# Decode attention with a gated feed-forward: TensorE's loop body as half a set used twice, with one value slot

## The chip, the cores and the metric

The kernel runs on one core of a Trainium2 chip. The metric is device time in microseconds of one execution; the median of three runs before the change is 195.83 us (195.80 to 195.85). One more execution was taken with the hardware profiler, and its page and trace are what the text quotes. Engines are named as on that page: PE (TensorE matmuls), PEld (its weight loads), DVE (VectorE), ACT (ScalarE), POOL (GpSimd), SP (SyncE, which only issues transfers here).

## The reference

Four batch rows, one token each. The output is a gate between sliding-window attention over a cache and a gated feed-forward:

```python
g = sigmoid((x * gate_w).sum(-1, keepdims=True))
# attention: 32 query heads, 8 key/value heads, the last W = 4096 of 16384 positions, Dh = 128
q = (x @ wq)                                  # per head
p = softmax(q @ k.T * Dh ** -0.5)             # over W positions
a = (p @ v) @ wo
# feed-forward, F = 1792
gate = x @ W_gate; up = x @ W_up
b = (gate * (gate > 0) * up) @ W_down
return g * a + (1 - g) * b
```

All inputs are bf16. The keys and values that are read are 4 batches x 8 heads x 4096 positions x 128 each, 32 MiB of keys and 32 MiB of values; with the weights the core reads 81 MB.

## The kernel before, in words

The work is cut into eight sets. A set is one batch and four key/value heads: its keys are one 4 MiB load, its values another. Loads go to `slots`, four buffers of 128 x 16384 bf16. `_dma_order` lists the loads as SP issues them, on one queue: wq, x, gate_w, k0, k1, v0, then k(s) and v(s-1) in turn, then the two feed-forward weights wg and wu (which share a slot), v7, wd, and wo in five pieces. `_slots` hands out the four buffers in rotation and notes what a load waits for: the last reader of what lay there before. A key slot is free when DVE has evicted score block 2 of its set (by then all four transposes have read it), a value slot after the value products `PV`. SP issues in order, so a load that waits holds up all loads behind it.

A set's work, with the names that the code uses:

- `KT(s, f)`, f = 0 to 3 (L555): DVE transposes a quarter of the keys from the slot into `kt`, which has four buffers of 128 x 4096, one for each f.
- `SC(s, f)`: TensorE makes a block of scores, 8 matmuls of 512 columns, into one of four PSUM banks (`SCB`), then DVE evicts the block with a running maximum (`ESC`, L591).
- after block 3: `MAX` and `SW` (a 32-column matmul) with `ESW` on DVE (L601) give the negated maximum; `EXP` on ACT (L694) makes the exponentials into `pe` with their sums.
- `PT(s)` (`EPT`, L606): DVE transposes them into `pT`, which has two buffers, used in turn.
- `PV(s)`: 32 matmuls of `pT` with the values, into one of two PSUM banks (`OB`), copied out by ACT (`NORM`, L679).

After the loop TensorE does the row sums (`RS`), the feed-forward's first products (`GU`), the last `PV`, then `FFN`, the mix of the heads (`OQ`) and the output projection `WO`, piece by piece as wo lands. All matmuls are recorded under one helper line, L306.

`_order` fixes one sequence of these steps, from which DVE's and ACT's programs are made. TensorE's program is written apart, as blocks with branches: a block `set` (score blocks 0 to 2 of a set), then `even` or `odd` (the value products of the set before, one copy for each value semaphore and `pT` buffer), then `rest` (score block 3 and `SW`); `setup` and `gates` are run once, `mix` and `tail` end it. TensorE waits for semaphores that DVE raises (`kt`, `mx`, `pt`), that ACT raises (`nm`) and that the value loads raise (`d_v0`, `d_v1`). In this order the value products of set s-1 stand between score blocks 2 and 3 of set s, and DVE does the first transpose of set s before it evicts block 3 of set s-1:

```python
for s in range(1, NSET):
    o += [("KT", s, 0), ("SC", s - 1, 3), ("SW", s - 1)]
    o += [("KT", s, 1), ("PT", s - 1), ("SC", s, 0), ("KT", s, 2), ("SC", s, 1), ("KT", s, 3)]
    o += [("SC", s, 2), ("PV", s - 1)]
```

Of the kernel before, what the change touches and what calls it, by code (L numbers as in the profile page):

```python
# [104 lines left out]
def _alloc(nc, ctx):  # L105
# [42 lines left out]
def _order():  # L148
    o = [("CONST", k) for k in ("mask", "grp", "rfold")] + [("XT",), ("Z",), ("Q",), ("QT",), ("KT", 0, 0), ("KT", 0, 1), ("SC", 0, 0)]
    o += [("KT", 0, 2), ("SC", 0, 1), ("KT", 0, 3), ("SC", 0, 2)]  # L150
    for s in range(1, NSET):
        o += [("KT", s, 0), ("SC", s - 1, 3), ("SW", s - 1)]
        o += [("KT", s, 1), ("PT", s - 1), ("SC", s, 0), ("KT", s, 2), ("SC", s, 1), ("KT", s, 3)]
        o += [("SC", s, 2), ("PV", s - 1)]
    s = NSET - 1
    o += [("SC", s, 3), ("SW", s), ("PT", s), ("RS", 0), ("RS", 1), ("GU",), ("PV", s), ("FFN",), ("OQ",)]
    return o + [("WO", p) for p in range(len(WO_PIECES))]
# [9 lines left out]
def _slots():  # L167

    frees = [[] for _ in range(NSLOT)]
    at, wait = {}, {}  # L170
    turn = 0
    for it in _dma_order():
        k = it[0]
        if k in ("x", "gw") or (k == "wo" and it[1] > 0):
            continue
        if k == "wu":
            at[it] = at[("wg",)]
            wait[it] = wait[("wg",)]
            continue
        n = turn % NSLOT  # L180
        turn += 1
        at[it] = n
        wait[it] = list(frees[n])
        frees[n] = {"k": [("E", "SC", it[-1], 2)], "v": [("PV", it[-1])], "wq": [("Q", 1)], "wg": [("GU", 1)], "wd": [], "wo": []}[k]
    return at, wait


def _program(nc, plan, R, aps):
    (A_x, A_k_cache, A_v_cache, A_wq, A_wo, B_W_gate, B_W_up, B_W_down, gate_w, out) = aps
    banks = [R["psum"][:, i, :] for i in range(8)]  # L190
# [29 lines left out]
    free = {("RS", 0): [("E", "SW", NSET - 1)], ("RS", 1): [("E", "SC", NSET - 1, 0)], ("GU", 0): [("E", "SC", NSET - 1, 1)],  # L220
            ("GU", 1): [("E", "SC", NSET - 1, 2)], ("OQ",): [("E", "SC", NSET - 1, 3)], ("Q", 0): [("INIT",)], ("Q", 1): [("INIT",)]}
    for i, key in enumerate(turns):
# [12 lines left out]

    def ob(s):
        return banks[OB[s % 2]]

    def sync(e):
# [5 lines left out]
        for it in _dma_order():  # L245
# [19 lines left out]
            else:  # L265
                b, qq = set_of(it[1])
                src = (A_k_cache if k == "k" else A_v_cache)[b, 4 * qq:4 * qq + 4, SK - WIN:SK, :]
                load((k.upper(), it[1]), f"d_{k}{it[1] % (3 if k == 'k' else 2)}", slot(*it), src.rearrange("h (r c) d -> r h (c d)", r=32),
                     waits=w)
# [32 lines left out]
    def tensor(t):  # L302
# [46 lines left out]
        def SC(s, f, s_at=0):  # L349
            key = ("SC", s, f)  # L350
            bk = banks[scb(key)]
            kv = kt[:, f, :].rearrange("p (t c h k e) -> p t c h k e", t=2, c=16, h=2, k=32)
            if plan.emit:
                E.take("kt", f + 1, 4 if f == 3 else 0)
            for t in range(2):
# [17 lines left out]
        def PV(s):  # L373
            vv = slot("v", s).rearrange("p (f t c d) -> p f t c d", f=4, t=2, c=16)
            if plan.emit:
                E.take("nm", 1, 1)
                E.take("pt", 1, 1)
                E.take(f"d_v{s % 2}", 16, 16)
            for f in range(4):
                for c in range(0, 16, 2):  # L380
                    x = 512 * f + 32 * c
                    r = 64 * (c // 2 % 2)
                    mm(ob(s)[r:r + 64, :], pT[:, s % 2, x:x + 64], vv[:, f, :, c:c + 2, :], (f, c) in ((0, 0), (0, 2)),
                       (f, c) in ((3, 12), (3, 14)), ev=("PV", s) if (f, c) == (3, 14) else None, pos=(0, r))

        def OQ():
            key = ("OQ",)
            if plan.emit:
                E.take("nm", 2)
            for t in range(2):  # L390
# [45 lines left out]
        if not plan.emit:  # L436
            setup()
            for s in range(NSET):
                for f in range(3):
                    SC(s, f)  # L440
                if s:
                    PV(s - 1)
                SC(s, 3)
                SW(s)
# [9 lines left out]

        at, odd = t.alloc_register("at"), t.alloc_register("odd")
        t.reg_mov(at, 0)
        t.reg_mov(odd, 1)
        t.sem_inc(plan.sems["nm"], 2)
        here = t.mark_branch_hint_location()
        t.br("pe_setup")  # L460
        with block("set"):
            sv = t.snap(at, min_val=0, max_val=NSET - 1)
            for f in range(3):
                SC(0, f, sv)
            t.br_eq(at, 0, on_true="pe_rest", on_false="pe_turn")
        with block("turn"):
            t.br_eq(odd, 0, on_true="pe_even", on_false="pe_odd")
        with block("even"):
            PV(0)
            t.br("pe_rest")  # L470
        with block("odd"):
            PV(1)
            t.br_eq(at, NSET, on_true="pe_mix", on_false="pe_rest")
        with block("rest"):
            SC(0, 3, t.snap(at, min_val=0, max_val=NSET - 1))
            SW(0)
            t.reg_add(at, at, 1)
            t.reg_alu(odd, odd, 1, op=ALU.bitwise_xor)
            t.br_lt(at, NSET, on_true="pe_set", on_false="pe_leave")
        with block("leave"):  # L480
            t.br("pe_gates")
        E.seen = {}
        with block("gates"):
            run("RS", "GU")
            t.br("pe_odd")
        E.seen = {}
        with block("setup"):
            setup()
            t.br("pe_set")
        E.seen = {}  # L490
# [55 lines left out]
    def vector(v):  # L546
        E = _Eng(plan, v, "dve")

        def INIT():
            E.op(lambda: v.memset(qblk[:, :, :, :, :].rearrange("p s h c e -> p (s h c e)"), 0.0), ev=("QZ",))  # L550
            E.op(lambda: v.memset(R["psum"][:, SCB[1]:ACC + 1, :].rearrange("p k c -> p (k c)"), 0.0), ev=("INIT",))

        def EKT(s, f):
            w = [("K", s)] + ([("SC", s - 1, f)] if s else [])
            E.op(lambda: v.transpose(kt[:, f, :].bitcast(FP32), slot("k", s)[:, 4096 * f:4096 * f + 4096].bitcast(FP32)),  # L555
                 ev=("E", "KT", s, f), waits=w, ctr="kt")
# [48 lines left out]
        def EPT(s):  # L605
            E.op(lambda: v.transpose(pT[:, s % 2, :], pe[:, :]), ev=("E", "PT", s), ctr="pt",  # L606
                 waits=[("EXP", s)] + ([("PV", s - 2)] if s >= 2 else [("XT",)]))

# [51 lines left out]
    def scalar(a):  # L660
# [17 lines left out]
        def NORM(s):  # L678
            E.op(lambda: a.activation(osb[:, s, :], ob(s), ACTF.Copy), ev=("NORM", s), ctr="nm",  # L679
                 waits=[("PV", s)])  # L680
# [53 lines left out]
```

## Time and profile before

| what | us |
|---|---|
| median of three runs | 195.83 |
| the profiled execution, its own time | 195.97 |
| its span, first to last instruction | 194.7 |
| DVE busy | 124.4 |
| PE busy | 124.0 |
| 32 key transposes on DVE | 73.7 |
| 256 score matmuls on PE | 72.0 |
| 256 value matmuls on PE | 32.3 |

The page gives busy time, then the span in 40 slices (busy tenths of each engine, the granted TensorE clock in tenths, the DMA engines' share, GB/s), the DMA queues, and the costliest groups. The timeline lists instructions in order of time: start, length, engine, line, operation, output and input, count, and in brackets the idle time ahead of it with what ended that. The windows give a row for each stretch: its bounds and length, then busy time and count for PE, PEld, DVE, ACT and POOL, then the granted clock, the DMA share and GB/s.

### The profile page before, as it was taken

The page shows a single profiled execution, that of the slowest core. Times are in us where ns is not written, and L with a number is a line of the kernel's source. Part 1 is how long each engine was busy: PE and PEld are TensorE (multiplying, and loading weights), DVE is VectorE, ACT ScalarE, POOL GpSimd, SP SyncE. Part 2 cuts the span into 40 slices and gives each one's busy share as a digit, 9 for nine tenths or more (in the row PEclk, how much of TensorE's full clock was granted, in tenths as well). Part 3 has the DMA queues.
Part 4 walks back from the last instruction along what each step waited for, and adds up shares of the span by engine and source line. Part 5 has one row for each costly group of instructions (what it writes and reads, how often), then busy time and mean ns, then how long its engine had stood idle before and what let it go on. Part 6 is the DMA issues. An engine that isn't in the chain of part 4 may idle for free. (4 is left out here: it accounts for less than half of the span.)

```text
span 194.7 us, 1963 instructions
## 1 busy us (share of the span) xinstructions
PE 124.0 (64%) x723; PEld 53.0 (27%) x723; DVE 124.4 (64%) x153; ACT 27.5 (14%) x34; POOL 9.6 (5%) x25
## 2 busy tenths in 40 slices
PE   0209257573966696579358627863886398764975
PEld 0004222131422242124113212321232133232563
DVE  6103688999489829991998099809980998253010
ACT  2213100040022004101310131013101300150100
POOL 7830000000000000000000000000000000000000
PEclk9999859998899579969999988995799669978699
DMA  6999999999999999999999999999999999998991
GB/s 222 427 439 438 431 431 431 451 438 438 431 431 431 431 431 438 431 438 431 431 438 431 438 431 431 431 431 438 431 431 431 431 385 424 477 438 380 432 396 58
DMA packets 3619, 81.03 MB, mean 416 GB/s; under 512 B 409, under 2 KB 674, under 8 KB 802
## 3 DMA queue, kind: packets, MB, share of 16 engines
q1 hardware_dynamic: 3618, 81.01, 97.2%
q8 instruction: 1, 0.02, 0.0%
HBM read 81.01 MB, written 0.00 MB: 416 GB/s over the span
## 5 line engine op out<-in xcount | busy, mean ns | idle before, releaser
L555 DVE STREAM_TRANSPOSE kt<-slots 128x2048 f32<-128x2048 f32 x32 | 73.7, 2305 | 25.1 <-DMA slots<-in_A_k_cache_dram 25.1
L306 PE MATMUL bank<-kt,qblk 128*128 128x512 bf16 x256 | 72.0, 432 | 27.6 <-DVE kt L555 22.5
L306 PEld LDWEIGHTS bank<-kt,qblk 128*128 x256 | 25.8, 107 | 69.4 <-issue 27.3
L306 PE MATMUL bank<-slots,pT 128*64 128x512 bf16 x256 | 32.3, 410 | 2.8 <-PEq L82 2.8
L591 DVE CUSTOM_DVE_ANT_0 sc<-bank,maskf 128x512 bf16<-128x512 f32 x32 | 21.1, 660 | 7.8 <-PE bank L306 7.8
L694 ACT ACTIVATE pe<-sc,negmax 128x2048 bf16<-128x2048 bf16 x8 | 16.0, 2002 | 50.4 <-DVE negmax L601 50.4
L306 PEld LDWEIGHTS bank<-slots,pT 128*64 128x64 bf16 x256 | 15.4, 118 | 20.5 <-issue 10.7
L606 DVE STREAM_TRANSPOSE pT<-pe 128x2048 bf16<-128x2048 bf16 x8 | 18.5, 2312 | 2.2 <-ACT pe L694 2.2
L679 ACT ACTIVATE osb<-bank 128x512 bf16<-128x512 f32 x8 | 4.8, 597 | 90.1 <-PE bank L306 90.1
L306 PE MATMUL bank<-rd,grpb 128*128 128x32 bf16 x8 | 1.4, 179 | 20.6 <-PEq L82 20.6
L306 PEld LDWEIGHTS bank<-rd,grpb 128*128 128x128 bf16 x8 | 0.8, 98 | 24.3 <-issue 24.3
L619 DVE TENSOR_TENSOR oq<-bank,recip 64x128 bf16<-64x128 f32 x2 | 0.9, 434 | 9.7 <-PE bank L306 9.7
L306 PE MATMUL bank<-slots,xT 128*4 128x512 bf16 (+1 forms) x64 | 6.5, 583 | 0.0
L559 DVE COPY xT<-bank 128x20 bf16<-128x20 bf16 x1 | 0.2, 170 | 7.7 <-PE bank L310 7.7
L306 PE MATMUL bank<-slots,oq 128*4 128x256 bf16 x64 | 4.3, 272 | 1.3 <-DVE oq L619 1.1
L581 DVE TENSOR_SCALAR qblk<-bank 32x64 uint32<-32x64 uint32 x16 | 2.9, 215 | 3.0 <-PE bank L310 2.9
L306 PE MATMUL bank<-maskr,maskl 128*128 128x512 bf16 x1 | 0.6, 606 | 5.9 <-POOL maskr L282 5.9
L310 PE MATMUL bank<-identb,xsb 5*128 5x5 bf16 x4 | 0.3, 167 | 5.6 <-DMA xsb<-in_A_x_dram 5.6
L306 PEld LDWEIGHTS bank<-slots,oq 128*4 128x4 bf16 x64 | 2.7, 84 | 2.9 <-DMA slots<-in_A_wo_dram 2.4
L282 POOL TENSOR_SCALAR_AFFINE_SELECT fold<-fold 128x256 bf16<-128x256 bf16 x8 | 3.4, 419 | 1.1
L641 DVE CAST xsb<-bank 4x256 bf16<-4x256 f32 x1 | 0.4, 419 | 4.7 <-PE bank L306 4.7
L601 DVE TENSOR_REDUCE negmax<-bank 128x1 f32<-128x32 f32 x8 | 1.5, 191 | 2.9 <-PE bank L306 2.9
(59 smaller groups left out, 42.3 us busy)
## 6 DMA issues: line engine op xcount, KB each, us to landing
slots<-in_A_k_cache_dram SPq DMA_DIRECT2D x8, 4096.0 KB, 24.1
slots<-in_A_v_cache_dram SPq DMA_DIRECT2D x8, 4096.0 KB, 30.6
slots<-in_A_wq_dram SPq DMA_DIRECT2D x1, 4096.0 KB, 13.6
slots<-in_A_wo_dram SPq DMA_DIRECT2D x1, 2240.0 KB, 21.1
slots<-in_B_W_gate_dram SPq DMA_DIRECT2D x1, 1792.0 KB, 19.0
slots<-in_B_W_up_dram SPq DMA_DIRECT2D x1, 1792.0 KB, 22.9
slots<-in_B_W_down_dram SPq DMA_DIRECT2D x1, 1792.0 KB, 17.9
slots<-in_A_wo_dram SPq DMA_DIRECT2D x1, 1088.0 KB, 23.4
```

The lines of the kernel that those rows point to most:

```text
L282: op(lambda: e.affine_select(dst, src, pattern, cmp, fill, base=base, channel_multiplier=mult), ev)
L306: E.op(lambda: t.matmul(out_, lhsT, rhs, start=start, stop=stop, tile_position=pos, skip_group_check=True), ev=ev, waits=waits)
L310: E.op(lambda: t.transpose(out_, in_, idn), ev=ev, waits=waits)
L555: E.op(lambda: v.transpose(kt[:, f, :].bitcast(FP32), slot("k", s)[:, 4096 * f:4096 * f + 4096].bitcast(FP32)), ev=("E", "KT", s, f), wait ...
L581: E.op(lambda dst=dst, r=r, g=g: v.tensor_scalar(dst, src[r, g, 0:B, :, :], 0, None, op0=ALU.bitwise_or), ev=("E",) + keys[1] if (q, g) == ...
L591: E.op(lambda: v.tensor_tensor_reduce(sc[:, 512 * f:512 * f + 512], banks[scb(key)], R["maskf"][:, :], 1.0, -3.0e38, ALU.add, ALU.max, mx4 ...
L601: E.op(lambda: v.tensor_reduce(negmax[:, s % 2:s % 2 + 1], banks[tr(key)][:, 0:32], AXIS.X, ALU.min), ev=("E",) + key, waits=[key])
L606: E.op(lambda: v.transpose(pT[:, s % 2, :], pe[:, :]), ev=("E", "PT", s), ctr="pt", waits=[("EXP", s)] + ([("PV", s - 2)] if s >= 2 else [ ...
L619: E.op(lambda g=g, r=r: v.tensor_tensor(oq[r, :, :].rearrange("p i b -> p b i"), banks[tr(key)][0:64, 128 * g:128 * g + 128].rearrange("p ...
L641: E.op(lambda: v.tensor_copy(osum[:, OW:2 * OW], banks[ACC][OR:OR + 4, 0:OW]), ev=("OSUM", 1), waits=[("WOP", len(WO_PIECES) - 1)])
L679: E.op(lambda: a.activation(osb[:, s, :], ob(s), ACTF.Copy), ev=("NORM", s), ctr="nm", waits=[("PV", s)])
L694: E.op(lambda: a.activation(pe[:, :], sc[:, :], ACTF.Exp, bias=negmax[:, s % 2:s % 2 + 1], scale=SCALE, accum_out=rowsum[:, s:s + 1]), ev= ...
```

## The change

TensorE's loop body becomes half a set: one block `half` with two score blocks, used twice for each set, with `value` (the value products) between the two halves. So `kt` has two buffers in place of four, the scores use two PSUM banks in place of four, `pT` has one buffer and the value products one accumulator bank. The value products of set s-1 stand ahead of score block 2 of set s, and DVE does the first transpose of set s after `SW` of set s-1. The fourth slot is for values alone and the other three go round among all other loads, so value load s waits for `PV(s-1)`; one semaphore `d_v` counts all value loads.

```diff
-    sb("kt", [128, 4, 4096], BF16)
+    sb("kt", [128, 2, 4096], BF16)
-    sb("pT", [128, 2, 2048], BF16)
+    sb("pT", [128, 2048], BF16)
...
-    o += [("KT", 0, 2), ("SC", 0, 1), ("KT", 0, 3), ("SC", 0, 2)]
+    o += [("KT", 0, 2), ("SC", 0, 1), ("KT", 0, 3), ("SC", 0, 2), ("SC", 0, 3), ("SW", 0)]
     for s in range(1, NSET):
-        o += [("KT", s, 0), ("SC", s - 1, 3), ("SW", s - 1)]
-        o += [("KT", s, 1), ("PT", s - 1), ("SC", s, 0), ("KT", s, 2), ("SC", s, 1), ("KT", s, 3)]
-        o += [("SC", s, 2), ("PV", s - 1)]
+        o += [("KT", s, 0), ("KT", s, 1), ("PT", s - 1), ("SC", s, 0), ("KT", s, 2), ("SC", s, 1), ("KT", s, 3), ("PV", s - 1)]
+        o += [("SC", s, 2), ("SC", s, 3), ("SW", s)]
...
-        n = turn % NSLOT
-        turn += 1
+        if k == "v":
+            n = NSLOT - 1
+        else:
+            n = turn % (NSLOT - 1)
+            turn += 1
...
-    TR, SCB, ACC, OB = (0, 1), (1, 2, 3, 4), 5, (6, 7)
+    TR, SCB, ACC, OB = (0, 1), (2, 3), 5, 6
...
-            bank_of[("SC", s, f)] = SCB[f]
+            bank_of[("SC", s, f)] = SCB[f % 2]
...
             if plan.emit:
-                E.take("kt", f + 1, 4 if f == 3 else 0)
+                E.take("kt", 1, 1)
...
-                E.take(f"d_v{s % 2}", 16, 16)
+                E.take("d_v", 16, 16)
...
+        with block("setup"):
+            setup()
+            t.br("pe_half")
         with block("turn"):
             SW(0)
             t.reg_add(at, at, 1)
+            t.br_lt(at, NSET, on_true="pe_half", on_false="pe_gates")
         with block("gates"):
             run("RS", "GU")
+            t.br("pe_value")
+        with block("half"):
+            sv = t.snap(at, min_val=0, max_val=NSET - 1)
+            for f in range(2):
+                SC(0, f, sv)
+            t.reg_alu(half, half, 1, op=ALU.bitwise_xor)
+            t.br_eq(half, 0, on_true="pe_turn", on_false="pe_first")
+        with block("first"):
+            t.br_eq(at, 0, on_true="pe_half", on_false="pe_value")
+        with block("value"):
+            PV(0)
+            t.br_lt(at, NSET, on_true="pe_half", on_false="pe_mix")
...
-            w = [("K", s)] + ([("SC", s - 1, f)] if s else [])
+            w = [("K", s)] + ([("SC", s, f - 2)] if f > 1 else [("SC", s - 1, f + 2)] if s else [])
...
-                 waits=[("EXP", s)] + ([("PV", s - 2)] if s >= 2 else [("XT",)]))
+                 waits=[("EXP", s)] + ([("PV", s - 1)] if s else []))
```

More of the change, by code (lines that the diff above doesn't have):

```diff
@@ L234, in set_of @@
         return s % 4, s // 4
-    def ob(s):
-        return banks[OB[s % 2]]
+    ob = banks[OB]
     def sync(e):
@@ L438, in tensor @@
             for s in range(NSET):
-                for f in range(3):
+                for f in range(4):
+                    if s and f == 2:
+                        PV(s - 1)
                     SC(s, f)
-                if s:
-                    PV(s - 1)
-                SC(s, 3)
                 SW(s)
@@ L453, in block @@
             return nc.body("pe_" + name, valid_engines=only)
-        at, odd = t.alloc_register("at"), t.alloc_register("odd")
+        at, half = t.alloc_register("at"), t.alloc_register("half")
         t.reg_mov(at, 0)
-        t.reg_mov(odd, 1)
-        t.sem_inc(plan.sems["nm"], 2)
+        t.reg_mov(half, 0)
+        t.sem_inc(plan.sems["nm"], 1)
         here = t.mark_branch_hint_location()
         t.br("pe_setup")
[L461 to L465, printed above, removed]
-        with block("turn"):
[L467 to L475, printed above, removed]
+        with block("setup"):
+            setup()
+            t.br("pe_half")
+        E.seen = {}
+        with block("turn"):
             SW(0)
             t.reg_add(at, at, 1)
[L478 to L481, printed above, removed]
+            t.br_lt(at, NSET, on_true="pe_half", on_false="pe_gates")
         E.seen = {}
```

29 lines of the change are left out of this document (12 added, 17 removed).

## The prediction

> **What bounds the kernel now.** I read the page's busy shares and slices first, then its DMA queues, then the windows, then the timeline around one set of the loop.
>
> ```profile
> span 194.7 us, 1963 instructions
> ...
> PE 124.0 (64%) x723; PEld 53.0 (27%) x723; DVE 124.4 (64%) x153; ACT 27.5 (14%) x34; POOL 9.6 (5%) x25
> ...
> PEclk9999859998899579969999988995799669978699
> DMA  6999999999999999999999999999999999998991
> ...
> q1 hardware_dynamic: 3618, 81.01, 97.2%
> q8 instruction: 1, 0.02, 0.0%
> ...
> slots<-in_A_k_cache_dram SPq DMA_DIRECT2D x8, 4096.0 KB, 24.1
> slots<-in_A_v_cache_dram SPq DMA_DIRECT2D x8, 4096.0 KB, 30.6
> ...
> slots<-in_B_W_gate_dram SPq DMA_DIRECT2D x1, 1792.0 KB, 19.0
> ```
>
> No engine is busy more than 64% of the span, while the 16 DMA engines are busy 97.2% of it, in every slice but the first and last few. The windows give the same by stage, and two short ones show the very end:
>
> ```profile
> 53.28:150.43 97.15, 66.72 (x343) 26.21 (x337) 70.32 (x76) 14.06 (x16) 0.00 (x0) 0.89 1.00 432
> 150.43:178.57 28.14, 17.40 (x102) 6.97 (x103) 19.67 (x27) 5.33 (x6) 0.00 (x0) 0.82 1.00 429
> ...
> 191.00:191.60 0.60, 0.60 (x16) 0.50 (x11) 0.00 (x0) 0.00 (x0) 0.00 (x0) 1.00 0.06 25
> 191.60:192.20 0.60, 0.60 (x12) 0.29 (x8) 0.00 (x0) 0.00 (x0) 0.00 (x0) 1.00 0.06 21
> ```
>
> The last two columns are DMA share and GB/s. Over five sets the share is 1.00 at 432 GB/s. In the last 1.2 us before 192.2 it is 0.06, one sixteenth: one DMA engine works alone, so every transfer lands when this late engine is done, and the other fifteen have over 1.2 us to spare. So the kernel's time is its bytes through the late engine, as long as the queue always holds the next transfer. A change in TensorE's order can cost something only where it lets that queue run dry. How far ahead the queue is filled is read from one set:
>
> ```profile
> 92.14 2.31 DVE L555 STREAM_TRANSPOSE kt<-slots 128x2048 f32<-128x2048 f32 x1 [4.37 <-DMA slots<-in_A_k_cache_dram]
> 94.37 0.65 DVE L591 CUSTOM_DVE_ANT_0 sc<-bank,maskf 128x512 bf16<-128x512 f32 x1
> ...
> 95.62 0.19 DVE L601 TENSOR_REDUCE negmax<-bank 128x1 f32<-128x32 f32 x1 [0.36 <-PE bank L306]
> 95.73 2.30 DVE L555 STREAM_TRANSPOSE kt<-slots 128x2048 f32<-128x2048 f32 x1
> ...
> 97.97 2.31 DVE L606 STREAM_TRANSPOSE pT<-pe 128x2048 bf16<-128x2048 bf16 x1
> ...
> 100.80 2.31 DVE L555 STREAM_TRANSPOSE kt<-slots 128x2048 f32<-128x2048 f32 x1
> 103.03 0.65 DVE L591 CUSTOM_DVE_ANT_0 sc<-bank,maskf 128x512 bf16<-128x512 f32 x1
> 103.16 1.91 PE L306 MATMUL bank<-kt,qblk 128*128 128x512 bf16 x8 [3.16 <-DVE kt L555]
> 103.61 2.31 DVE L555 STREAM_TRANSPOSE kt<-slots 128x2048 f32<-128x2048 f32 x1
> 105.00 3.64 PE L306 MATMUL bank<-slots,pT 128*64 128x512 bf16 x32
> ...
> 106.53 0.53 SPq L243 DMA_DIRECT2D slots<-in_A_k_cache_dram  x1
> 108.68 0.53 SPq L243 DMA_DIRECT2D slots<-in_A_v_cache_dram  x1
> 111.57 2.31 DVE L555 STREAM_TRANSPOSE kt<-slots 128x2048 f32<-128x2048 f32 x1 [5.07 <-DMA slots<-in_A_k_cache_dram]
> ```
>
> Keys land at about 92.14 and 111.57, 19.43 us apart, one key and one value load of equal size (4096 KB each by the issue rows), so a value load lands about 9.7 us behind its keys. At 106.53 and 108.68 the SP queue issues the loads that follow, while the key load landing at 111.57 and a value load landing about 121.3 are still under way: the queue is filled some 13 us ahead.
>
> **The change part by part.** Call T the landing of a set's keys.
>
> *One value slot.* Value load s now waits for the products of set s-1, and all loads behind it on SP's queue (the next keys, in the end wg, wu, wd, wo) wait with it. In the old order it waited for the products two sets back. The new key loads wait for a set three back and are never last. The step is nothing if the value products end early enough ahead of T+19.43, when the next keys are through. With the rows above, DVE does first and second transposes, pT, then eviction and transpose twice. A transpose is 2.23 from start to start (100.80 to 103.03), an eviction 0.58 (103.03 to 103.61): kt 0 and 1 until T+4.5, pT until T+6.7, kt 2 until T+9.5, kt 3 until T+12.3. TensorE does score blocks 0 and 1 by T+6.5 (1.91 each) and then waits for values: they land at T+9.7. Products 3.64: T+13.4. Score blocks 2 and 3 now stand behind them: T+17.2. From the last eviction to the end of negmax is 1.4 (94.37 to 95.73): T+18.6. That is 0.8 short of 19.43, so DVE is back in time for the next keys, with one accumulator bank (its copy runs while TensorE waits anyway) and one pT (needed again only at T+19.43+4.5).
>
> The next value load is issued at T+13.4, 6.0 us ahead of the end of the keys under way. How long a load needs to start isn't shown; the output's bounds it:
>
> ```profile
> 193.43 0.29 SPq L243 DMA_DIRECT2D out_dram<-xsb  x1
> ```
>
> From that issue to the end of the span are 1.3 us, landing included. So the lead falls from 13 to 4.7 us, but not to zero: 0 us lost per set.
>
> *Half clock.* A second cost could come from TensorE's clock, in tenths in the PEclk row. One block of scores and the products are seen slow as well:
>
> ```profile
> 47.32 3.29 PE L306 MATMUL bank<-kt,qblk 128*128 128x512 bf16 x8 [3.16 <-DVE kt L555]
> ...
> 178.57 5.33 PE L306 MATMUL bank<-slots,pT 128*64 128x512 bf16 x32 [2.82 <-PEq L82]
> ```
>
> A score block rises from 1.91 to 3.29, the products from 3.64 to 5.33, at worst twice 3.64 = 7.3. With 7.3 a value load is issued at T+17.0 and runs by T+18.3: still ahead of T+19.43. [...]
>
> *The first hand-over is the tight one.* Set 0 has no values to wait for, and DVE is behind the keys there:
>
> ```profile
> 33.49 2.31 DVE L555 STREAM_TRANSPOSE kt<-slots 128x2048 f32<-128x2048 f32 x1
> ...
> 36.10 1.91 PE L306 MATMUL bank<-kt,qblk 128*128 128x512 bf16 x8 [1.15 <-PEq L82]
> 36.30 2.31 DVE L555 STREAM_TRANSPOSE kt<-slots 128x2048 f32<-128x2048 f32 x1
> 36.41 0.54 SPq L243 DMA_DIRECT2D slots<-in_A_v_cache_dram  x1
> ...
> 51.38 0.53 SPq L243 DMA_DIRECT2D slots<-in_A_k_cache_dram  x1
> 53.28 2.31 DVE L555 STREAM_TRANSPOSE kt<-slots 128x2048 f32<-128x2048 f32 x1 [1.93 <-DMA slots<-in_A_k_cache_dram]
> ```
>
> Value load 1 went out at 36.41. Now: kt 3 of set 0 ends at 35.8, score block 3 at 37.9, negmax at 39.4. Only then come the transposes of set 1 (one of them ran at 36.30): until 43.9, pT until 46.2, products 46.3 to 49.9. Value load 1 goes out at 50.0 and runs by 51.3; the keys ahead of it (set 2) end at 53.28. That leaves 2.0 us: cost 0. If score blocks 0 and 1 of set 1 both run at 3.29 (41.7 to 48.3), the products end between 52.0 and 53.7, the load runs by 53.3 to 55.0, and 0 to 1.7 us are lost once. I take 0.1, nearer to the full clock, since TensorE worked at 36 and works from 41.7 on.
>
> *Fewer instructions, other jumps.* Counted in the code, with a weight load for each matmul, TensorE's program shrinks from 647 instructions to 538; a set takes five branches for four, and a score block takes its semaphore down by itself. A set's TensorE time has no share in the sum, so these cost 0; without that cover some 0.1 us a set.
>
> *The tail.* The last value load (behind wg and wu) is issued at 150.43+13.4 = 163.8; the queue holds v6, wg and wu until about 150.4+9.7+8.5 = 168.6 (wg and wu at 1792 of 4096 KB each take 4.25). wo moves to the slot of the last keys and waits for score block 2 (about 166) instead of the products:
>
> ```profile
> 164.84 0.33 SPq L243 DMA_DIRECT2D slots<-in_B_W_down_dram  x1
> ...
> 166.98 2.23 SPq L243 DMA_DIRECT2D slots<-in_A_wo_dram  x5
> ...
> 190.78 2.15 PE L306 MATMUL bank<-slots,oq 128*4 128x256 bf16 x29 [0.20 <-DMA slots<-in_A_wo_dram]
> ```
>
> Both were and are issued far ahead of the last value landing (178.5, where the products start at 178.57). The last matmuls still wait for the last piece of wo: 0.
>
> **Sum.** The profiled execution took 195.97 us (span 194.7 and 1.3 around it), 0.14 above the median of three. 195.97 + 0 + 0.1 = 196.07, against the median 195.83 + 0.1 = 195.9.
>
> **Rivals.**
> - B, the first hand-over runs dry (slower). TensorE's products of set 0 end after 52.0 because of the half clock, as worked out above; it decides from an issue of value load 1 later than 52.0. For it: the 3.29 of the old block at 47.32. Against: denser work there now. Price 0.4 to 1.7, so 196.2 to 197.5; 196.6 as the likeliest, since both blocks would have to be slow throughout for more.
> - C, the value slot binds in every set (slower). A set loses what its products end later than T+18.1 (19.43 less 1.3). It needs half clock through the products and both score blocks behind them: products until T+17.0, blocks until T+23.6, negmax T+25.0, 5.6 behind the next keys; pT is then ready 12.3 behind them, and products of 7.3 end at 19.6, 1.5 late. For it: the slow rows above. Against: the window 53.28:150.43 has a mean clock of 0.89 (third column from the end), so that half clock lasts a fifth of the time and not through. At 0.4 to 1.5 us for six sets it gives 198 to 205.
> - D, the program is fetched once more. The q8 row has one instruction transfer in the whole execution. The windows show one engine alone for 1.2 us at the end, and if that transfer put it back, another one would add about as much: 197.1. For it: the new loop stands in the middle of the program, the old one at its start. Against: the old program also jumped from gates near its middle back to its start and on to its end, and one transfer did.
> - E, the program is not fetched at all (faster). With 109 instructions fewer, the q8 transfer might not be needed; the late engine would be late no more, and at least 1.2 us, say 1.4, fall away: 194.4. Against: the last instructions stay far from the first ones.
> - F, that single buffers in kt or banks hold up DVE: block 2's transpose waits for block 0's matmuls, done by T+4.3, long before T+7.3. It gives the forecast's time and is part of it.
>
> [...]
>
> **How the numbers follow.** Forecast A (queue never dry, 195.8 to 196.2): 0.43. B 0.20, C 0.08, D 0.09, E 0.20. A bound of 0.2% is 0.39 us, about what a measurement of this kernel can tell from no change. Slower by more: B, C and D, 0.37; within: A, 0.43; faster: E, 0.20. The range reaches from E's 194.4 to 197.2, which takes in B but for its far end and D, and leaves C and little else out. A's own range is 195.7 to 196.2.
>
> **What would show it.** Value loads issued about T+13.4 (lead 4.7 us after the start) with DMA share 1.00 in the windows between 53 and 178, keys still 19.43 apart, products starting where values land, and set 1's value load out at 50.0 show A right. Key landings from set 3 on shifted by one constant, with a window below 1.00 near 53, would be B; a stretched spacing, C. A q8 row of 2, or none, would be D or E. The forecast is wrong at its root if the DMA share falls below 97% while the bytes stay.

## The result, and the profile after

| | before | after |
|---|---|---|
| median, us (20 runs each, same chip) | 195.98 | 197.21 |
| lowest and highest, us | 195.67, 196.54 | 195.82, 198.67 |
| the profiled execution, us | 195.97 | 197.25 |
| its span, us | 194.7 | 196.0 |

The ratio after to before is 1.0058, with an interval of 1.0037 to 1.0080: the changed kernel is slower by more than the 0.2% that can be told apart. 195.83 × 1.0058 = 197.0 lies inside the stated range (the bare median of 197.21 stands on its upper edge, 197.2), but the likeliest case (195.9) did not come. What came looks like rival B. Here and below a ratio leaves out runs more than 1.5% above the fastest of their kernel (six of the 14 of `warm`, one each of `warm_once`, `wd_early` and the kernel before), while the medians count all.

Compare not only the medians: the runs before lie within 0.9 us of each other, those after within 2.9 us. The two lowest of the 20 (195.82 and 195.85) are as fast as the old kernel. So the question is not only what costs about 1.3 us in the profiled execution, but why some executions are spared.

The page of the changed kernel, its first lines, DMA slices, queues and the issue rows with the time from issue to landing at the end:

```profile
span 196.0 us, 2003 instructions
...
PE 125.8 (64%) x723; PEld 56.4 (29%) x723; DVE 124.7 (64%) x153; ACT 27.5 (14%) x34; POOL 9.5 (5%) x25
...
DMA  6999999999599999999999999999999999999994
GB/s 214 441 442 448 435 438 428 448 428 428 214 421 448 435 435 428 428 428 428 428 428 428 428 428 428 428 428 428 428 428 428 455 420 430 447 441 395 433 409 156
...
q1 hardware_dynamic: 3618, 81.01, 96.7%
q8 instruction: 1, 0.02, 0.0%
...
slots<-in_A_k_cache_dram SPq DMA_DIRECT2D x8, 4096.0 KB, 24.8
slots<-in_A_v_cache_dram SPq DMA_DIRECT2D x8, 4096.0 KB, 15.6
slots<-in_A_wq_dram SPq DMA_DIRECT2D x1, 4096.0 KB, 12.3
```

The engines' busy times are as before to 2 us, but for the weight loads (PEld 56.4, before 53.0), which overlap the matmuls. The bytes are the same, and there is still one instruction transfer. One thing is new: the eleventh slice (49.0 to 53.9 us) has a DMA digit of 5 and 214 GB/s where its neighbours have 428 and 421. A value load now goes out 15.6 us ahead of its landing in place of 30.6, as one slot must give. The windows around that slice, and over the stages that the prediction looked at (busy time and count of PE, PEld, DVE, ACT, POOL; then TensorE's granted clock, DMA share, GB/s):

```profile
51.40:53.40 2.00, 2.00 (x13) 0.80 (x10) 0.42 (x1) 0.60 (x1) 0.00 (x0) 1.00 0.23 66
53.40:55.40 2.00, 1.88 (x9) 0.67 (x7) 0.78 (x3) 0.00 (x0) 0.00 (x0) 1.00 1.09 459
55.40:151.60 96.20, 65.45 (x326) 28.15 (x326) 71.45 (x79) 14.22 (x16) 0.00 (x0) 0.86 1.00 431
151.60:179.60 28.00, 16.98 (x101) 7.33 (x101) 18.72 (x23) 4.57 (x6) 0.00 (x0) 0.76 1.00 428
```

The queue is dry once, for about two microseconds. After that it is full for 124 us at 428 to 431 GB/s, like before: in this execution no later set loses anything, although TensorE's clock is lower in those stages (0.86 and 0.76, where they had 0.89 and 0.82). The timeline says how it comes to the gap and what follows from it:

```profile
42.12 6.01 PE L305 MATMUL bank<-kt,qblk 128*128 128x512 bf16 x16 [2.75 <-PEq L82]
48.06 3.64 PE L305 MATMUL bank<-slots,pT 128*64 128x512 bf16 x32
51.74 0.54 SPq L242 DMA_DIRECT2D slots<-in_A_v_cache_dram  x1
...
73.96 4.51 DVE L548 STREAM_TRANSPOSE kt<-slots 128x2048 f32<-128x2048 f32 x2 [0.66 <-DMA slots<-in_A_k_cache_dram]
...
93.39 4.50 DVE L548 STREAM_TRANSPOSE kt<-slots 128x2048 f32<-128x2048 f32 x2 [0.87 <-DMA slots<-in_A_k_cache_dram]
96.06 6.34 PE L305 MATMUL bank<-kt,qblk 128*128 128x512 bf16 x16 [3.77 <-PEq L82]
103.21 3.64 PE L305 MATMUL bank<-slots,pT 128*64 128x512 bf16 x32 [0.81 <-PEq L82]
106.89 0.53 SPq L242 DMA_DIRECT2D slots<-in_A_v_cache_dram  x1
...
112.81 2.31 DVE L548 STREAM_TRANSPOSE kt<-slots 128x2048 f32<-128x2048 f32 x1 [0.87 <-DMA slots<-in_A_k_cache_dram]
```

The first two rows are set 1's score blocks 0 and 1 and the value products of set 0. The 16 score matmuls take 6.01 us where they take 3.8 at full clock (twice 1.91). The products end at 51.7, and value load 1, which now waits for them, is issued at 51.74. From there on the keys land at 73.96, 93.39 and 112.81: still 19.4 apart, but 1.25 later than before (92.14 and 111.57 there). That shift is carried unchanged to the end: the span is 1.3 longer. What is slow at 42.12 is TensorE's clock, as windows of 3.4 us show:

```profile
36.70:40.10 3.40, 1.55 (x8) 0.50 (x6) 1.59 (x5) 0.47 (x1) 0.00 (x0) 1.00 0.89 386
40.10:43.50 3.40, 1.38 (x4) 0.62 (x5) 3.40 (x2) 1.62 (x2) 0.00 (x0) 0.51 1.03 443
43.50:46.90 3.40, 3.40 (x10) 1.15 (x9) 3.40 (x5) 0.00 (x0) 0.00 (x0) 0.50 1.07 463
46.90:50.30 3.40, 3.40 (x28) 1.54 (x28) 3.40 (x4) 0.00 (x0) 0.00 (x0) 0.99 1.07 463
```

In 36.70:40.10 TensorE works 1.55 us of 3.40. Then the clock is halved for two such windows, although TensorE is busy throughout the second. The third is back at 0.99.

### The profile page after: what moved, and what is told of

It reads as the page before. It is cut to its first block, busy times and chain, and to the rows that moved or that the text cites. A ratio compares the mean times of both kernels' runs of the same rounds, so it can differ in the third digit from the quotient of the medians.

```text
span 196.0 us, 2003 instructions
## 1 busy us (share of the span) xinstructions
PE 125.8 (64%) x723; PEld 56.4 (29%) x723; DVE 124.7 (64%) x153; ACT 27.5 (14%) x34; POOL 9.5 (5%) x25
## 3 DMA queue, kind: packets, MB, share of 16 engines
q1 hardware_dynamic: 3618, 81.01, 96.7%
## 5 line engine op out<-in xcount | busy, mean ns | idle before, releaser
L305 PE MATMUL bank<-kt,qblk 128*128 128x512 bf16 x256 | 75.0, 455 | 30.6 <-PEq L82 30.6
L548 DVE STREAM_TRANSPOSE kt<-slots 128x2048 f32<-128x2048 f32 x32 | 72.9, 2297 | 4.2 <-DMA slots<-in_A_k_cache_dram 4.1
L305 PEld LDWEIGHTS bank<-kt,qblk 128*128 x256 | 27.8, 111 | 74.2 <-issue 57.3
L305 PE MATMUL bank<-slots,pT 128*64 128x512 bf16 x256 | 31.0, 397 | 10.9 <-PEq L82 10.9
L305 PEld LDWEIGHTS bank<-slots,pT 128*64 128x64 bf16 x256 | 16.8, 114 | 25.4 <-issue 16.8
L687 ACT ACTIVATE pe<-sc,negmax 128x2048 bf16<-128x2048 bf16 x8 | 16.0, 2002 | 50.7 <-DVE negmax L594 50.7
## 6 DMA issues: line engine op xcount, KB each, us to landing
slots<-in_A_v_cache_dram SPq DMA_DIRECT2D x8, 4096.0 KB, 15.6
slots<-in_A_wq_dram SPq DMA_DIRECT2D x1, 4096.0 KB, 12.3
```

Source lines behind the costliest of these rows:

```text
L305: E.op(lambda: t.matmul(out_, lhsT, rhs, start=start, stop=stop, tile_position=pos, skip_group_check=True), ev=ev, waits=waits)
L548: E.op(lambda: v.transpose(kt[:, f % 2, :].bitcast(FP32), slot("k", s)[:, 4096 * f:4096 * f + 4096].bitcast(FP32)), ev=("E", "KT", s, f), ...
L687: E.op(lambda: a.activation(pe[:, :], sc[:, :], ACTF.Exp, bias=negmax[:, s % 2:s % 2 + 1], scale=SCALE, accum_out=rowsum[:, s:s + 1]), ev= ...
```

## The experiments

The theory after this comparison (H in the expectations below): the single value slot makes value load 1 wait for the products of set 0, these come late because the half clock falls on set 1's score blocks, the queue runs dry once, and all that follows is shifted. Against it stood: that the slot costs in every set and only the profiled execution hides it (S); that the later instruction transfer (F), the new loop of half sets or the single buffers cost something; and that the half clock is there but decides nothing. Ratios are to the kernel before, run beside each on the same chip.

| run | edit to the changed kernel | median, us | ratio | interval |
|---|---|---|---|---|
| `two_slots` | two value slots again | 195.96 | 0.9998 | 0.9982 to 1.0014 |
| `first_free` | value load 1 alone needn't wait | 196.06 | 1.0002 | 0.9980 to 1.0024 |
| `warm_once` | nine idle matmuls after set 0's maximum | 196.03 | 1.0002 | 0.9981 to 1.0024 |
| `warm` | the same in every set | 198.73 | 1.0084 | 1.0053 to 1.0114 |
| `delay_once` | 16 idle matmuls ahead of the first products | 199.68 | 1.0204 | 1.0152 to 1.0257 |
| `delay` | 8 ahead of the products of every set | 202.74 | 1.0326 | 1.0280 to 1.0371 |
| `wd_early` | wd loaded early, a buffer of its own | 199.85 | 1.0195 | 1.0156 to 1.0233 |
| `small` | TensorE's program cut to 446 instructions | 199.91 | one run | |
| `again` | none | 196.17 | one run | |
| `one_slot_old` | the kernel *before* with one value slot | 204.02 | 1.0384 | 1.0340 to 1.0428 |

**Is it the slot?** `two_slots` gives the value loads two slots and leaves all else as changed (TensorE's loop body of half a set with two copies of the products, two key buffers, two score banks, one accumulator, one `pT`).

```diff
-        if k == "v":
-            n = NSLOT - 1
-        else:
-            n = turn % (NSLOT - 1)
-            turn += 1
+        n = turn % NSLOT
+        turn += 1
...
-                E.take("d_v", 16, 16)
+                E.take(f"d_v{s % 2}", 16, 16)
...
```

> The changed kernel with two value slots, as before the change: slots in rotation, two copies of the value products, two value semaphores; the half-set loop, two key buffers, two score banks, one pT and one accumulator bank stay. Theory H and rival S: the queue is filled 13 us ahead again, value load 1 goes out near 36.5, ratio 0.999 to 1.002 with little scatter. Rival F, or a cost of the half-set loop itself: ratio stays near 1.006.

The ratio is 0.9998. Its timeline has the same slow score blocks, but the value load is long gone by then:

```profile
36.29 0.54 SPq L239 DMA_DIRECT2D slots<-in_A_v_cache_dram  x1
...
41.74 6.00 PE L302 MATMUL bank<-kt,qblk 128*128 128x512 bf16 x16 [2.75 <-PEq L82]
```

So the half clock alone costs nothing that shows beyond 0.2%, and neither do the jumps, the single buffers or the order; only the slot's wait makes the half clock matter. F goes with it: the DMA records have the instruction transfer at 27.4 us here, as late as in the changed kernel.

**Is it the first hand-over only?** `first_free` keeps the single slot from value load 2 on and gives value 0 a slot of its own, which the key loads share later.

```diff
-            n = NSLOT - 1
+            n = 1 if it[1] else 3
         else:
-            n = turn % (NSLOT - 1)
+            n = (0, 1, 2, 0, 3, 2, 0, 3, 2, 0, 3, 2)[turn]
             turn += 1
...
```

> The changed kernel in which only value load 1 gets a slot of its own (free once score block 2 of set 0 is evicted, as before the change); value loads 2 to 7 still share one slot, each waiting for the products of the set before. Theory H (the cost arises at the first hand-over alone): value load 1 goes out near 36.5, keys of set 3 land at 72.7 to 73.1, ratio 0.999 to 1.002. Rival S (the single slot costs a little in every set): five of the six costs stay, ratio 1.004 to 1.006.

The ratio is 1.0002: with the first hand-over free, the single slot of the other six costs nothing that can be measured. The issues of value loads 1 and 2 in its timeline:

```profile
36.92 0.54 SPq L242 DMA_DIRECT2D slots<-in_A_v_cache_dram  x1
...
68.51 0.54 SPq L242 DMA_DIRECT2D slots<-in_A_v_cache_dram  x1
```

Its profiled execution (span 195.4) does show a slice of 315 GB/s at 68 to 73 us, and the keys of set 4 are 0.7 us late (92.83, before 92.14), although value load 2 went out 4.2 us ahead of the landing of the keys under way (72.66). So the second hand-over can be short too, at a cost of some tenths, and one of the twelve runs was long (197.85).

**Is it the half clock?** `warm_once` fills TensorE's pause after set 0's maximum, once, with nine matmuls into a bank that nobody reads (idle matmuls, in the table). `warm` does the same in every set, and was run first.

```diff
         with block("turn"):
             SW(0)
             t.reg_add(at, at, 1)
+            t.br_eq(at, 1, on_true="pe_warm", on_false="pe_next")
+        with block("warm"):
+            for _ in range(9):
+                mm(banks[7], R["grpb"][:, :], R["maskf"][:, :], True, True)
+            t.br("pe_half")
+        with block("next"):
```

> The changed kernel with nine more matmuls once, after the maximum of set 0, so that set 1's score blocks start at full clock; nothing is added in later sets. Theory H with the half clock as its cause: value load 1 goes out at 49.4 to 50.1 in place of 51.74, ratio 0.999 to 1.003, and most runs within 0.5 us of the kernel before. If value load 1 is late with full clock too (a load needs more lead than the 1.3 us of the prediction), ratio 1.003 to 1.006 with value load 1 out by 50.1 all the same.

```profile
39.87 1.89 PE L305 MATMUL bank<-maskf,grpb 128*128 128x512 bf16 x8 [0.32 <-issue]
42.30 3.93 PE L305 MATMUL bank<-kt,qblk 128*128 128x512 bf16 x16 [0.54 <-PEq L82]
46.73 3.64 PE L305 MATMUL bank<-slots,pT 128*64 128x512 bf16 x32 [0.49 <-PEq L82]
50.40 0.54 SPq L242 DMA_DIRECT2D slots<-in_A_v_cache_dram  x1
...
72.66 4.51 DVE L554 STREAM_TRANSPOSE kt<-slots 128x2048 f32<-128x2048 f32 x2 [0.87 <-DMA slots<-in_A_k_cache_dram]
```

More work on TensorE makes the changed kernel faster: with 1.9 us of idle matmuls the two score blocks take 3.93 in place of 6.01, the load goes out at 50.40 in place of 51.74, set 3's keys are there at 72.66 in place of 73.96, and the ratio falls from 1.0058 to 1.0002. That is the cause by its other end. Two of the twelve runs were still long (197.79 and 198.83).

> The changed kernel with nine more matmuls after each set's maximum (128x512, into an unused bank, of constants), so that TensorE stays busy while it waits for the next transposes. Theory H (one late hand-over: score blocks 0 and 1 of set 1 ran at half clock, so value load 1 went out at 51.74 and the queue ran dry once near 52): set 1's blocks start at full clock, value load 1 goes out by 50.5, keys of set 3 land at 72.7 as before the change in place of 73.94, time within 0.3 us of the kernel before (ratio 1.000 to 1.002), and the runs scatter less than the 2.9 us of the changed kernel. Rival S (the single slot costs a little in every set): time stays 0.6% above. Rival F (the instruction transfer, now at 29 us in place of 6 us, costs the 1.2 us): stays 0.6% above, too.

`warm` missed. Its value load 1 goes out early too, but its ratio is 1.0084. Its profiled execution is the longest of its 14 runs (202.46), so its rows show what can happen, not what is usual:

```profile
41.33 3.93 PE L305 MATMUL bank<-kt,qblk 128*128 128x512 bf16 x16 [0.80 <-PEq L82]
...
49.38 0.54 SPq L242 DMA_DIRECT2D slots<-in_A_v_cache_dram  x1
...
164.13 5.33 PE L305 MATMUL bank<-slots,pT 128*64 128x512 bf16 x32 [3.47 <-PEq L82]
```

The idle matmuls of each set keep the score blocks at full clock (3.93 us above), but then TensorE pauses 3.47 us for the values and the half clock falls on the products, 5.33 us in place of 3.64; in this execution that happens to five of the seven in the loop. Those are the last work ahead of a hand-over, so the delay goes straight into the load. It is not the whole loss: the keys of set 3 land at 74.19 here, 1.5 us later than in `warm_once`, although their hand-over was early. A load's landing is recorded in sixteen parts; fifteen of value load 1 are there by 61.80 and the last at 64.20. Why that part came so late isn't shown.

**What does a late issue cost?** `delay_once` puts 16 idle matmuls (3.4 us) ahead of the products of set 0, once.

```diff
-            t.br_eq(at, 0, on_true="pe_half", on_false="pe_value")
+            t.br_eq(at, 0, on_true="pe_half", on_false="pe_pick")
+        with block("pick"):
+            t.br_eq(at, 1, on_true="pe_late", on_false="pe_value")
+        with block("late"):
+            for _ in range(16):
+                mm(banks[7], R["grpb"][:, :], R["maskf"][:, :], True, True)
+            t.br("pe_value")
         with block("value"):
```

> The changed kernel with sixteen more matmuls (128x512, into an unused bank; 3.5 us at full clock) ahead of the value products of set 0 alone. Theory H with the size that the other runs gave (a load that goes out onto a dry queue lands 12.5 us after its issue, and the kernel loses what value load 1 is issued after 50.4): value load 1 goes out between 53.5 and 55.3, all later landings move by issue less 50.4, 3.1 to 4.9 us, and stay 19.4 apart; span 197.8 to 199.6, ratio 1.016 to 1.025. If the later hand-overs take part, more than 1.025.

The ratio is 1.0204, as the theory expects; the span is 197.9. Value load 1 and the keys of set 3 in its timeline:

```profile
53.71 0.54 SPq L242 DMA_DIRECT2D slots<-in_A_v_cache_dram  x1
...
75.81 4.50 DVE L554 STREAM_TRANSPOSE kt<-slots 128x2048 f32<-128x2048 f32 x2 [0.53 <-DMA slots<-in_A_k_cache_dram]
```

`again` is the changed kernel once more, for a second profile of it.

> The changed kernel once more, for a second profile of it. Theory H: its span is 194.7 us and what value load 1 is issued after 50.4 us, within 0.3 us, whatever the issue time is this time (seen before: 51.74 and 196.0).

```profile
41.63 5.29 PE L305 MATMUL bank<-kt,qblk 128*128 128x512 bf16 x16 [2.75 <-PEq L82]
46.84 3.64 PE L305 MATMUL bank<-slots,pT 128*64 128x512 bf16 x32
50.42 3.65 PE L305 MATMUL bank<-kt,qblk 128*128 128x512 bf16 x16
50.52 0.53 SPq L242 DMA_DIRECT2D slots<-in_A_v_cache_dram  x1
...
72.89 4.50 DVE L548 STREAM_TRANSPOSE kt<-slots 128x2048 f32<-128x2048 f32 x2 [0.80 <-DMA slots<-in_A_k_cache_dram]
```

This is an execution that was spared: the half clock took only 1.5 us from the same 16 matmuls (5.29), they began 0.5 us earlier, and the load went out at 50.52. The trace's clock records have one step of 3.41 us at half clock here (41.59 to 45.01) and two in the first profile (40.15 to 46.97). Four profiles now lie on one line:

| run | value load 1 issued | keys of set 3 | span |
|---|---|---|---|
| `warm_once` | 50.40 | 72.66 | 194.7 |
| `again` | 50.52 | 72.89 | 194.9 |
| after | 51.74 | 73.96 | 196.0 |
| `delay_once` | 53.71 | 75.81 | 197.9 |

From 50.4 on each microsecond of a later issue is one of a longer span: 194.7 + (issue − 50.4) gives 194.8, 196.0 and 198.0 for the last three. `warm` is not on it, for the late part above and its later sets.

**Is it the program in TensorE's memory?** `small` makes the output projection in 32 matmuls of 512 columns in place of 64 of 256, and the feed-forward's last product in 14 in place of 28, which cuts TensorE's program from 538 to 446 instructions. It was to show whether the instruction transfer goes away (rival E).

```diff
-OUTT = 2
+OUTT = 1
...
-WO_PIECES = ((0, 35), (35, 52), (52, 59), (59, 62), (62, 64))
+WO_PIECES = ((0, 18), (18, 26), (26, 30), (30, 31), (31, 32))
...
```

> The changed kernel with feed-forward and output projection in matmuls of 512 columns in place of pairs of 256 (OUTT = 1), and one copy of the output by DVE: 92 TensorE instructions fewer, 446 in all. It asks whether the one instruction transfer goes away with a shorter program (rival E), not for its time: the longer matmuls stand in the tail and make it 2 to 4 us longer. If the transfer depends on the program's length, the q8 row has none and no DMA engine ends later than the others; if it comes whenever TensorE leaves the first part of its program, q8 stays at 1.

```profile
q8 instruction: 1, 0.02, 0.0%
```

The transfer stays, so a program of five sixths of the length does not buy E. The 199.91 itself is the new tail's and says nothing of the change.

**Does products ahead of block 2 matter?** `one_slot_old` takes the old kernel and gives it one value slot and nothing else.

```diff
-        n = turn % NSLOT
-        turn += 1
+        if k == "v":
+            n = NSLOT - 1
+        else:
+            n = turn % (NSLOT - 1)
+            turn += 1
```

> The kernel before with the change's slot plan alone: one slot for values, all else old (value products behind score block 2, four key buffers and banks). Theory H: value load 1 waits for products that end near 54.1, goes out dry, lands some 12.5 us later (as long as the first load took from its issue), at 66.7 in place of 63.0: 3.7 us once, 199.7 us, ratio 1.019. If the later leads (products until T+16.5, 2.9 us ahead) are too short as well, up to 1 us in each of six sets more: up to 205 us.

The ratio is 1.0384, and the median of 204.02 lies near the far end (205) of what was expected, not at its main figure of 199.7. Two windows of it:

```profile
51.40:55.40 4.00, 4.00 (x31) 1.83 (x28) 2.31 (x1) 0.60 (x1) 0.00 (x0) 1.00 0.26 66
111.00:119.00 8.00, 3.17 (x21) 1.15 (x17) 3.56 (x6) 0.84 (x2) 0.00 (x0) 0.95 0.92 356
```

Here the first gap is twice as long, and later sets have one too. In the old order the products stand behind block 2, and value load 1 went out at 53.97, 2.2 us later than in the changed kernel; with them ahead of it the single slot is nearly affordable (0.6% in place of 3.8%). The two kernels differ in the buffers and in DVE's order as well; that the place of the products alone makes the difference was not tested.

**Two that missed.** `delay` holds up the products of every set by eight idle matmuls (1.7 us).

```diff
                 E.take("d_v", 16, 16)
+                for _ in range(8):
+                    mm(banks[7], R["grpb"][:, :], R["maskf"][:, :], True, True)
```

> The changed kernel with eight more matmuls (128x512, into an unused bank) between the wait for the values and the value products, so that every set's products end about 1.7 us later at full clock. Theory H: set 1 pays it in full, once, since its load was late already: the keys of set 3 land 1.5 to 2.2 us later than 73.94, later sets stay 19.4 apart, so ratio about 1.013 to 1.018 (198.5 to 199.5 us). Rival S: every set's lead was used up, so 6 to 8 times 1.7 us come on top, 207 us or more. If the lead of the later sets is what the prediction says (4.7 us), nothing beyond set 1.

The ratio of 1.0326 lies between the two numbers. Its first issue is at 52.06, worth 1.7 by the line above, and it lost some 6.4 (0.0326 × 196). With the loads issued 15 to 16 us behind the keys in place of 13.5, later hand-overs are late in part, and the last products, in the tail, are held up too. Against the kernel before, its keys of set 3 land 1.5 us late (74.17, there 72.69), those of set 7 2.9 (153.26, there 150.40), the work behind the last values starts 5.5 late (184.03, there 178.57), and the span is 6.8 longer. The later leads are no idle reserve.

`wd_early` loads wd right behind the third set of keys into a buffer of its own, which was meant to give the queue something to do during the gap.

```diff
-        o += [("k", s), ("v", s - 1)]
+        o += [("k", s)] + [("wd",)] * (s == 2) + [("v", s - 1)]
...
```

> The changed kernel with wd loaded between the keys of set 2 and value load 1 into a buffer of its own, so that 4.25 us more of transfers lie ahead of value load 1; the order of TensorE and the single value slot stay. Theory H: the queue doesn't run dry even with set 1 at half clock (value load 1 is due at about 57 and goes out by 53.7); ratio 0.999 to 1.002, and little scatter. Rival S: the single slot still binds in every set, ratio stays near 1.006. Rival F: stays near 1.006.

The ratio is 1.0195. The gap did go (value load 1 went out at 50.37 in this execution, with wd under way until 57.5), but wd had been covering something else. The end of its timeline:

```profile
182.75 5.26 PE L306 MATMUL bank<-slots,pT 128*64 128x512 bf16 x32 [3.98 <-PEq L82]
...
192.57 3.66 PE L306 MATMUL bank<-slots,oq 128*4 128x256 bf16 x64 [1.07 <-DVE oq L613]
...
196.73 0.29 SPq L243 DMA_DIRECT2D out_dram<-xsb  x1
```

The transfers end as early as in the kernel before, but the last products start 4.2 us later than there (182.75 against 178.57), since the last values now come behind wd, with only wo behind them. From the last products to the output's issue are 14 us of work, and now that work ends last: the output projection waits for DVE's `oq`, no longer for wo.

No version was faster than the kernel before; `two_slots`, `first_free` and `warm_once` equal it.

## Why the prediction was right and wrong

- **The bound was right.** Transfers end last, and TensorE's order costs only where the queue runs dry. All of the 1.3 us in the profile comes from one dry stretch. It takes the queue's share from 97.2% to 96.7%, under the 97% that the prediction named as a sign against itself.
- **The timeline of a set was right.** Predicted: products where values land, next value load at T+13.4, keys 19.43 apart. Measured with T = 93.39: the products at T+9.8, the load at T+13.5, the next keys 19.42 later, and a DMA share of 1.00 from 55.4 to 179.6. The 0 per set holds in the profile of the changed kernel, and over the runs of `first_free`. The lead of 4.7 us was too large, though: with the start of a load as measured below (2.9 ahead of the keys' end) it is 19.4 − 13.5 − 2.9 = 3.0, if the 2.9 holds for later sets. It does not always: in `delay`, value loads issued at 109.03 and 128.86, each 4.1 us ahead of the landing of the keys under way, cost 0.4 and 0.9 us (the keys behind them land 19.8 and 20.4 us after those). What sets the lead that is needed stays open.
- **Half clock per set: right in its sum, not in its reason.** The prediction let the products be slow (7.3 us) and found the load still early enough. In the profile the half clock falls on the score blocks: the slow blocks at 96.06 (6.34) end before the values land, and the products at 103.21, like all in the loop, run at full clock. With a load's start as measured below, slow products would not have been free: the load at T+17.0 would be 2.4 us ahead of the next keys, less than 2.9.
- **The first hand-over was wrong, and this decided it.** The step said: products 46.3 to 49.9, load out at 50.0, "I take 0.1, nearer to the full clock, since TensorE worked at 36 and works from 41.7 on". Work shortly before and after was not enough: the half clock took 2.2 us from set 1's blocks, which began at 42.12 in place of 41.7, and the load went out at 51.74. The bounds stood in the prediction and the choice between them was the error. The windows show it: 1.55 us of matmuls in 36.70:40.10 did not prevent the half clock (0.51 and 0.50 in the next two), and full clock came back only behind 43.50:46.90, the first full window (0.99 follows).
- **The point from which it costs was mis-sized.** The prediction let a load run 1.3 us after its issue, from the output's 4 KB, and so put the deciding point at 52.0. By that term an issue at 51.74 would have cost nothing. Measured, it is about 50.4 (the least of the four that was seen, with the span of before), 1.6 us earlier. A 4 MiB load that meets an empty queue takes longer: wq, the first load of the kernel, lands 12.3 us after its issue (its row above), and the DMA records have value load 1 landed at 64.2, 12.5 after its issue, where a load in the full stream takes 9.7. The difference, 2.6 to 2.8, ahead of the keys' end at 53.28 gives 50.5 to 50.7. The page of before had a row of this kind, with wq at 13.6, and the prediction passed it over for a smaller transfer.
- **B's price came out, its condition did not.** Stated 0.4 to 1.7; the profile has 1.3. But B was to decide from an issue later than 52.0, and at 51.74 its own sum gives 0. It had the slow score blocks right and the start of a load too short; that a price inside its range came of both is partly luck.
- **The late engine was right, and it did something unforeseen.** By the slice of 214 GB/s the dry stretch is worth (428 − 214) / 428 × 4.9 = 2.45 us, but only 1.3 were lost. The rest was already lost before: one engine worked alone for the last 1.2 us (a DMA share of 0.06). Behind the dry queue all sixteen parts of a load land together again. The landing records show it: before, fifteen parts of value load 1 are there by 61.64 and the last at 62.98; in the changed kernel by 64.11 and at 64.23, so the fifteen lost 2.5 us and the last 1.25. The end looks different, too, in the windows of the changed kernel:

```profile
192.80:193.40 0.60, 0.60 (x11) 0.27 (x8) 0.00 (x0) 0.00 (x0) 0.00 (x0) 1.00 0.52 176
193.40:194.00 0.60, 0.60 (x10) 0.16 (x6) 0.00 (x0) 0.00 (x0) 0.00 (x0) 1.00 0.00 0
```

  From half of the engines at work to none, without the stretch of 0.06. So about the first 1.2 us of a dry queue are free in this kernel: `warm_once` dips to 283 GB/s in one slice and has the span of before.
- **C, D, E.** The spacing of the keys did not stretch (against C, though `delay` and `one_slot_old` show that later sets can lose, too). The q8 row stays at one transfer, in `small` too (against D and E).
- **Instructions, branches and tail at 0: right**, by `two_slots` at 0.9998, which has more branches than the changed kernel. The tail of the changed kernel only carries the shift on: its last products start at 179.79, 1.2 us later than before.

The scatter follows the clock. Of the 20 runs after, the eight with a mean granted clock of 0.844 or 0.852 have spans of 195.8 to 196.9, the twelve at 0.860 or more have 194.6 to 195.5 but for two (196.2 and 196.4). One more step of 3.4 us at half clock is 0.5 × 3.4 / 195 = 0.009 of the mean, the distance between those groups. That agrees with the two profiles, where set 1's blocks meet one such step or two. Spans of 195.8 or more came in ten of the 20 runs, in two of twelve of `warm_once`, one of twelve of `first_free` and none of twelve of `two_slots`; so most of the scatter goes with the first hand-over and some with the later ones. How much stays open, since only two executions of the unmodified changed kernel were profiled.

## What to carry to other kernels

Where a buffer is given up and its load then waits for a product, look for the one hand-over with the least lead (here the first, ahead of which TensorE has no values to wait for), not the typical one, and cost it at TensorE's half clock (here 6.01 us for two score blocks in place of 3.8). For the start of a load take the row of a load of the same size onto an empty queue, not a small one, and leave some reserve: in `delay` 4.1 us were not always enough. Before a transfer is moved to fill a gap, ask which work it covers where it stands.

## What the runs showed of the hardware that was not expected

- A window that was nearly half busy was followed by the half clock (1.55 of 3.40 us, then 0.51), and one with a little more work was not. The same two windows of `warm_once`:

```profile
36.70:40.10 3.40, 1.97 (x11) 0.80 (x10) 1.52 (x7) 0.29 (x1) 0.00 (x0) 1.00 0.94 405
40.10:43.50 3.40, 2.86 (x14) 1.25 (x13) 3.40 (x2) 1.81 (x2) 0.00 (x0) 1.00 0.98 424
```

  With 1.97 us and then 2.86 the clock stays at 1.00. Taken in steps of 3.41 us, the clock records of the profiles before and after show this: the full-clock steps that half clock follows have 1.52 us of matmuls or less, those that full clock follows 1.63 or more; the half-clock steps that full clock follows have 2.70 or more, those that half clock follows 2.35 or less. In the profiled execution of `warm` the same matmuls in every set moved the half clock onto the work that counts.
- Behind the one instruction transfer the last of a load's sixteen parts lands 1.1 to 1.4 us after the others, in the profiles before and after, until the queue runs dry. In the kernel before, the DMA records have that transfer (16 KiB) at 6.5 us, inside the wq load; in the changed kernel it comes at 29.2 us. The issue row of wq before, against 12.3 after:

```profile
slots<-in_A_wq_dram SPq DMA_DIRECT2D x1, 4096.0 KB, 13.6
```

  That is 1.3 us more for the same load, about the time for which one engine works alone at the end. Before, fifteen parts of wq are there by 13.10 and the last at 14.41. In the changed kernel wq is whole at 13.12, and it is the keys of set 1, under way at 29.2, that have a late part (33.57, the others by 32.51). The delay stays: before, to the last load (192.61, the others by 191.33); in the changed kernel, to the keys of set 2 (52.99, the others by 51.93), until value load 1 behind the dry queue has 0.12. Work waits for the last part: before, the keys of set 2 have fifteen by 51.93 and the last at 53.26, and the transposes begin at 53.28. That the transfer put one engine back is the author's estimate from these times; no run was without it, so its price by itself wasn't shown.
- An execution's time is mostly 1.2 to 1.3 us above its span, but in some runs of most of these kernels, the old one too, 1.9 to 2.7 (three of the 20 after, such as 197.33 with a span of 194.9). What lies there no profile shows.
